# One ring of four PSUM banks, scores through SBUF and grouped exponentials in an attention and two-layer kernel on one Trainium2 core

## The chip, the core and the metric

The kernel runs on one core of a Trainium2 chip. A core has five engines that run side by side, each with its own queue of instructions in a fixed order: PE (matrix products, into PSUM), ACT (activation functions), DVE (elementwise and reductions), POOL (elementwise, SBUF only) and SP, which here only issues DMAs. PSUM has eight banks of 128 x 512 floats. The metric is the device time of one execution in microseconds, the median of the runs shown; less is better.

## What is computed

Landmark attention for 4 batches of 8 heads (576 tokens, head size 64, 32 landmarks), then two dense layers on its 2304 x 512 output:

```python
A  = softmax(q @ k_lm^T / 8)      # 576 x 32 for each head
Bm = softmax(q_lm @ k_lm^T / 8)   # 32 x 32
C  = softmax(q_lm @ k^T / 8)      # 32 x 576
Z  = Bm^T / (norm1(Bm) * norminf(Bm))
for _ in range(6): Z = 2 * Z - Z @ Bm @ Z
x  = A @ Z @ C @ v                # q_lm, k_lm: means over 18 tokens
h  = x @ w_in;  x = (h * cos(h)) @ w_out             # 512 -> 2048 -> 512
h  = x @ w_in2; out = (max(h, 0) + alpha * min(h, 0)) @ w_out2
```

## The kernel before, in words

**A planner sets the order.** Every step is entered with `op(...)`: the engines that may do it, its buffers, an optional due time. `Plan.go` then places all steps by its own table of durations; where a step may go to two engines (a copy to ACT or DVE, a subtraction to POOL or DVE) it chooses. A step whose function table on ACT (`aset`: "exp" or "sin") is not the loaded one costs it 1.28 more and a later due time. The result is a fixed order on each engine. Buffers of one tag form a ring: a new one waits until the one that many places ahead in the ring is done with.

**Attention.** A batch is two units of four heads (`unit`, names `u0`, `u1` for batch 0, `U2` to `U7` after it). For each unit: k, q and v are loaded (batches 1 to 3 into `raw`, a ring of three that the loads of the layers' weights share); k and q are transposed on PE (L594); landmark sums go on POOL (L646) and are written into `kq`. The scores of C (L670 into two banks, 320 and 256 columns) are reduced to a maximum on DVE (L685, L687), and ACT takes their exponential straight from PSUM in two instructions (L692). C is transposed (L700, L704), copied to SBUF (L318 on ACT or L320 on DVE) and multiplied with v (L715). The scores of A (L670 too) are transposed by DVE (L742), reduced (L747), subtracted, sent through the exponential (L749), normalised and split into a hi and a lo part (L455, L323). `z_path` does Bm, its exponential (L800), and five Newton steps (L851 on PE, L853 on DVE) for the whole batch; its result `wt`, times `w_in`, gives V' (L909, hi part L911, lo part L912).

**First layer, a tick at a time.** Batch, half (288 tokens) and a slice of 128 of the 2048 columns make one of 128 ticks. A tick is six h1 products (L949) into one bank of tag `h`; ACT rounds (L954), DVE takes the rest (L956), ACT takes Sin (L958) and Square (L959), DVE multiplies by h (L960), which frees the bank; then a hi and a lo part (L963, L323) and twelve y1 products (L976) in four groups of three, into `acc`. The hi and lo parts have four buffers, so that h1 is at most some four ticks, 16 groups, ahead of y1. Ticks 0 to 15 belong to batch 0, 16 to 31 to batch 1, 32 to 63 to both again, 64 to 95 to batch 2, 96 to 127 to batch 3. The attention of batches 0 and 1 runs in the prologue, that of batch 2 is entered at tick 36 and that of batch 3 at tick 66. Beside all that DVE converts the weights from 64-bit to 32-bit floats (L471, L473, L475).

**Second layer.** Products by a Strassen scheme (L1235), for the last 256 tokens plain (L1280), and a second product (L1316).

**PSUM.** Tag `h` has two banks (h1, and half of the attention of batch 0), `x` two (the rest of the attention, V'), `acc` four. Sin and the exponential belong to different tables on ACT; each change is an ACT_TABLE_LOAD.

## Time and profile before

| | us |
|---|---|
| median of 3 runs | 882.39 (881.43 to 885.32) |
| the profiled execution | 881.18 |
| its span, first to last instruction | 879.4 |
| busy: PE, DVE, ACT, POOL | 825.8, 646.4, 483.9, 198.2 |

Busy times of an engine are counted per stretch of the span; a stretch in which PE is busy all the time can still hold products that take longer than in another. The rows on which the prediction rests stand in a section of their own below.

### The profile page before, as it was taken

The numbers are of one execution on the slowest core, as the hardware profiler recorded it, in microseconds if no ns is written. First come the engines' busy times: TensorE is split into PE (matmuls) and PEld (weight loads), VectorE is DVE, ScalarE is ACT, GpSimd is POOL, SyncE is SP. The second block draws the span as 40 slices with busy tenths as digits, with TensorE's granted clock in tenths as the row PEclk, the third lists the DMA queues.
The fourth block names the chain that finished last, engine by engine and source line by source line (L and its number), as shares of the span: only waits on it lengthen the run. The fifth ranks groups of instructions, "written<-read, shape, count | busy, mean of one in ns | idle before, by whom it ended". The sixth has DMA issues, their size and how long they took to land.

```text
span 879.4 us, 15395 instructions
## 1 busy us (share of the span) xinstructions
PE 825.8 (94%) x5681; PEld 726.3 (83%) x5681; DVE 646.4 (74%) x1279; ACT 483.9 (55%) x1118; POOL 198.2 (23%) x220
## 2 busy tenths in 40 slices
PE   5677899999999998999989999999999999999997
PEld 4436789888798887897889888889999999999996
DVE  4989969987896889768998777775665566555563
ACT  4467757777875687667678534443344334333431
POOL 1224511333321332114432222200120012000110
PEclk8989999999999999999999999999999999999999
DMA  8476506775359846666555111140113011310231
GB/s 233 116 215 143 171 26 189 229 178 136 123 159 268 230 119 196 186 182 218 182 185 181 51 48 48 61 132 25 37 61 85 25 37 60 85 37 25 66 115 24
DMA packets 89051, 107.44 MB, mean 122 GB/s; under 512 B 35984, under 2 KB 63120, under 8 KB 88976
## 3 DMA queue, kind: packets, MB, share of 16 engines
q1 hardware_dynamic: 88976, 106.46, 41.2%
q8 instruction: 44, 0.72, 0.3%
q14 instruction: 31, 0.25, 0.1%
HBM read 82.06 MB, written 24.38 MB: 121 GB/s over the span
## 4 chain that ended last, share of the span: by engine, by line
PE 61%; DVE 19%; DMA 10%; issue 3%; ACT 3%; SPq 1%; POOL 1%; DVEq 0%; POOLq 0%; ACTq 0%
PE acc L1316 21%; PE acc L976 10%; PE h L1235 9%; PE x L1235 7%; PE h L949 5%; DMA m<-in_moe_w_in_dram 4%; DMA m<-in_moe_w_out_dram 3%; DVE m L323 3%; DVE m L475 3%; DVE m L473 3%; PE x L909 2%; DMA m<-wi2d 2%; DVE m L471 2%; DVE m L960 2%; DVE m L956 2%
## 5 line engine op out<-in xcount | busy, mean ns | idle before, releaser
L976 PE MATMUL acc<-m,m 128*128 128x288 f32 x1536 | 238.0, 301 | 7.0 <-DVE m L323 3.4
L323 POOL TENSOR_TENSOR m<-m,m 128x288 fp32r<-128x288 f32 (+3 forms) x129 | 126.0, 984 | 459.7 <-ACT m L963 233.5
L976 PEld LDWEIGHTS acc<-m,m 128*128 128x128 f32 x1536 | 213.7, 190 | 18.4 <-issue 7.7
L1316 PE MATMUL acc<-m,m 128*128 128x512 f32 x864 | 207.5, 392 | 0.7 <-DVE m L323 0.4
L323 DVE TENSOR_TENSOR m<-m,m 128x512 fp32r<-128x512 f32 (+4 forms) x271 | 170.3, 651 | 34.9 <-ACT m L1184 9.3
L1316 PEld LDWEIGHTS acc<-m,m 128*128 128x128 f32 x864 | 158.9, 189 | 31.9 <-DVE m L323 0.9
L949 PE MATMUL h<-m,m 128*128 128x288 f32 x768 | 131.8, 307 | 14.9 <-DVE m L960 12.8
L949 PEld LDWEIGHTS h<-m,m 128*128 128x128 f32 x768 | 109.6, 191 | 34.9 <-DVE m L960 19.9
L1304 ACT ACTIVATE m<-m 128x512 fp32r<-128x512 f32 (+1 forms) x80 | 46.3, 588 | 111.5 <-DVE m L1302 109.0
L1235 PE MATMUL h<-m,m 128*128 128x256 f32 x768 | 106.9, 282 | 0.7 <-ACT m L318 0.6
L1235 PEld LDWEIGHTS h<-m,m 128*128 128x128 f32 x768 | 99.7, 189 | 3.6 <-ACT m L318 1.3
L1258 DVE TENSOR_TENSOR m<-h,m 128x512 f32<-128x512 f32 x32 | 22.1, 690 | 81.8 <-ACT m L318 78.9
L1235 PE MATMUL x<-m,m 128*128 128x256 f32 x576 | 80.3, 283 | 1.7 <-ACT m L318 1.7
L963 ACT ACTIVATE m<-m 128x288 fp32r<-128x288 f32 x128 | 55.8, 441 | 40.5 <-DVE m L960 35.4
L1235 PEld LDWEIGHTS x<-m,m 128*128 128x128 f32 x576 | 73.1, 188 | 3.4 <-ACT m L318 1.9
L318 ACT ACTIVATE m<-h 128x256 f32<-128x256 f32 (+2 forms) x93 | 36.8, 396 | 67.2 <-PE h L1235 58.9
L958 ACT ACTIVATE m<-m 128x288 f32<-128x288 f32 x128 | 55.6, 440 | 26.4 <-DVE m L956 26.0
L960 DVE SCALAR_TENSOR_TENSOR m<-m,h 128x288 f32<-128x288 f32 x128 | 56.5, 446 | 15.1 <-ACT m L959 14.8
L1095 ACT ACTIVATE m<-m 128x512 fp32r<-128x512 f32 x68 | 41.4, 628 | 45.0 <-PE h L1235 19.4
L954 ACT ACTIVATE m<-h 128x288 int32<-128x288 f32 x128 | 51.4, 404 | 22.8 <-PE h L949 22.0
L956 DVE SCALAR_TENSOR_TENSOR m<-h,m 128x288 f32<-128x288 f32 x128 | 57.0, 448 | 3.4 <-ACT m L954 3.2
L959 ACT ACTIVATE m<-m 128x288 f32<-128x288 f32 x128 | 55.2, 439 | 2.4
(150 smaller groups left out, 897.5 us busy)
## 6 DMA issues: line engine op xcount, KB each, us to landing
m<-in_moe_w_in_dram SPq DMA_DIRECT2D x32, 512.0 KB, 5.4
m<-in_moe_w_out_dram SPq DMA_DIRECT2D x32, 512.0 KB, 4.4
m<-wi2d SPq DMA_DIRECT2D x56, 256.0 KB, 3.5
...
```

What stands on the lines that cost most here:

```text
L323: ENG[e].tensor_tensor(o, a, b, op=ALU.subtract)
L949: nc.tensor.matmul(out=hp.t[:, 0:CW], lhsT=w_[:, js], rhs=x[:, cs], start=(i == 0), stop=(i == 5))
L954: op(act(CW, True), lambda e: nc.scalar.activation(k_.t, hp.t[:, 0:CW], AF.Copy, scale=INV2PI), r=[hp], w=[k_], target=T + 0.8)
L956: op(dve(CW), lambda e: nc.vector.scalar_tensor_tensor(u.t, hp.t[:, 0:CW], INV2PI, k_.t, op0=ALU.mult, op1=ALU.subtract), r=[hp, k_], w=[u])
L958: op(act(CW), lambda e: nc.scalar.activation(u.t, u.t, AF.Sin, scale=math.pi), rw=[u], aset="sin")
L959: op(act(CW), lambda e: nc.scalar.activation(u.t, u.t, AF.Square, scale=math.sqrt(2.0)), rw=[u])
L960: op(dve(CW), lambda e: nc.vector.scalar_tensor_tensor(hc.t, u.t, 1.0, hp.t[:, 0:CW], op0=ALU.subtract, op1=ALU.mult, reverse0=True), r=[h ...
L963: op(act(CW), lambda e: nc.scalar.activation(gh.t, hc.t, AF.Copy), r=[hc], w=[gh, gl])
L976: nc.tensor.matmul(out=yg[o].t[:, 0:CW], lhsT=w_.t[:, sl], rhs=x.t, start=(j == ja and i == 0), stop=(j == jb and i == 2),)
L1235: nc.tensor.matmul(out=rv(k), lhsT=a_.t[:, p, c2, js], rhs=b_.t[:, q_, c2, 0:hw], start=(first and c2 == 0 and i == 0), stop=(c2 == 1 and ...
L1304: op(act(w), lambda e, m_=m_, gh=gh: nc.scalar.activation(gh.t[:, 0:w], m_.t[:, 0:w], AF.Copy), r=[m_], w=[gh, gl])
L1316: nc.tensor.matmul(out=ya[n][t].t, lhsT=gv(x_), rhs=r_.t, start=(st and k == 0), stop=(en and k == 2))
```

## The change

Four things are edited.

1. **PSUM.** Tags `h` and `x` become one tag `h` with four banks. The C scores and A scores of batch 0 stay in `acc`.
2. **C scores of batches 1 to 3.** Each of the two score banks is copied to SBUF (ACT or DVE) into `ce`; one reduction on DVE then takes the negated maximum of all 576 columns (L703 in the new file) and one ACT instruction the exponential in place (L705). `ce` of these batches has two buffers in place of one; for that `wt` has two in place of four.
3. **Two groups of exponentials.** For each batch from 1 on, the exponential of C of the first unit waits for the maximum of the second and for the subtraction in `z_path`; that of C of the second waits for the first; that of A of the first waits for A's subtraction in the second. v of the first unit is loaded after k and q of both.
4. **The planner.** A step that needs the other table and is not overdue gets 1.0 added to the key by which it is chosen (`SP`).

```diff
 KN = dict(..., AG=8, SP=1.0, KA=0.004, KC=25, DRY=0)
...
                     key = s + KA * min(dl - s, KC)
+                    if o.aset and o.aset != cur and o.dl > s:
+                        key += KN["SP"]
...
-    at = at_raw = lay(0, at, ("wt", 4, 1024))
+    at = at_raw = lay(0, at, ("wt", 2, 1024), ("cex", 1, CE))
...
-    for tag, n in (("h", 2), ("x", 2), ("acc", 4)):
+    place["1ce"] = (1, CE, place["1ce"][2] + place.pop("cex")[2])
+    for tag, n in (("h", 4), ("acc", 4)):
...
-        bank = (lambda i: psb("hx"[i & 1])) if m == 0 else (lambda i: psb("x"))
-        pair = (lambda: (psb("acc"), psb("acc"))) if m == 0 else (lambda: (psb("x"), psb("x")))
+        bank = (lambda i: psb("h")) if m == 0 else (lambda i: psb("h"))
+        pair = (lambda: (psb("acc"), psb("acc"))) if m == 0 else (lambda: (psb("h"), psb("h")))
...
-        loads(4, ldv, 1.64, w=[vn], after=aft)
+        marks["vl", b, c] = loads(4, ldv, 1.64, w=[vn], after=aft)
...
+            if m:
+                ce = ce or atb(m, "ce", [P, R0, 2, 64])
+                op(pe(n, 4), cs, r=[kt, kqb[p][1]], w=[sc[ch]])
+                op([act(n, True), dve(n)], lambda e, ch=ch, n=n: copy(
+                    e, ce.t[:, 0:n // 64, ch, :], sc[ch].t[:, 0:n].rearrange("p (r s) -> p r s", s=64)),
+                   r=[sc[ch]], w=[ce])
+                continue
...
+            marks["cn", b, c] = op(dve(S), lambda e: nc.vector.tensor_reduce(
+                nm_.t, ces(), axis=AX.X, op=ALU.max, negate=True), r=[ce], w=[nm_])
+            marks["ce", b, c] = op(("ACT", S / 1200.0 + 0.18), lambda e: nc.scalar.activation(
+                ces(), ces(), AF.Exp, bias=nm_.t, accum_out=sm.t[:, 0:1]), r=[nm_], rw=[ce], w=[sm], aset="exp")
...
-        pv = psb("x")
+        pv = psb("h")
...
         z_path(b, tick_time(s + KN["UZ"]))
+        marks["vl", b, 0].after += gates["ld"]
+        marks["ce", b, 0].after += [marks["cn", b, 1], marks["zs", b]]
+        marks["ce", b, 1].after += [marks["ce", b, 0]]
+        marks["et", b, 1].after += [marks["et", b, 0]]
+        marks["vl", b, 1].after += [marks["vl", b, 0]]
+        marks["ae", b, 0].after += [marks["as", b, 1]]
         gates["v"] = [g.ops[-1]]
...
-        X, Y = psb("h"), psb("x")
+        X, Y = psb("h"), psb("h")
```

What the planner makes of it is shown at three places. In the rows L numbers are lines of each file's own; in the new file L705 and L774 are the exponentials of C and A, L825 that of z, L979, L983, L984 and L988 rounding, Sin, Square and hi part of a tick, L936 the hi part of V', L320 copies, L974 and L1001 h1 and y1.

ACT, before, near tick 50, from the second unit's C (L692) to z's exponential (L800) and on to A's (L749):

```order
L692 ACT_TABLE_LOAD
L692 ACTIVATE m_175,m_69<-x,m_69 128x5x64
L692 ACTIVATE m_175,m_69<-x,m_69 128x4x64
L954 ACTIVATE m_479<-h 128x288
L958 ACT_TABLE_LOAD
L958 ACTIVATE m_479<-m_479 128x288 x2
L959 ACTIVATE m_479<-m_479 128x288 x2
L318 ACTIVATE m_157<-x 64x128
L800 ACT_TABLE_LOAD
L800 ACTIVATE m_69<-m_69 128x64
L911 ACTIVATE m_1253<-x 128x512
```

The first unit's exponentials stood some six ticks ahead of these, between loads of their own. ACT, after, in the same place:

```order
L705 ACT_TABLE_LOAD
L705 ACTIVATE m_170,m_69<-m_170,m_69 128x576
L774 ACTIVATE m_69<-m_69 128x576
L705 ACTIVATE m_434,m_69<-m_434,m_69 128x576
L825 ACTIVATE m_69<-m_69 128x64
L774 ACTIVATE m_69<-m_69 128x576
L936 ACTIVATE m_1269<-h 128x512 x2
L983 ACT_TABLE_LOAD
L983 ACTIVATE m_483<-m_483 128x288
L459 ACTIVATE m_447<-m_1107 128x576
L984 ACTIVATE m_483<-m_483 128x288
L320 ACTIVATE m_69<-m_69 32x2x32 x4
```

All five exponentials of the batch stand in one piece, and the copies of C's transposes (128x512) stand behind the last row. In the whole order the table loads go from 24 to 12: from 6 to 8 in the prologue, from 10 to 2 near tick 50, from 8 to 2 near tick 80.

PE, before, behind h1 of ticks 79 and 80 (L779 is z's product, L700 and L704 the transposes of C, L670 scores, L715 C times v):

```order
L779 MATMUL x<-m_69 32x32 x8
L976 MATMUL acc<-m_504,m_1795 128x288 x3
L700 MATMUL x<-m_69,m_175 128x128 x4
L976 MATMUL acc<-m_504,m_1795 128x288 x6
L704 MATMUL x<-m_69,m_175 64x128
L976 MATMUL acc<-m_504,m_1795 128x288 x6
L670 MATMUL x<-m_175,m_69 64x320 x2
L670 MATMUL x<-m_175,m_69 64x256 x2
L976 MATMUL acc<-m_504,m_1795 128x288 x6
L715 MATMUL x<-m_157 32x64 x20
```

PE, after, behind h1 of tick 80 (L804 is z's product, L721 and L725 the transposes of C, L674 scores, L736 C times v):

```order
L1001 MATMUL acc<-m_519,m_1830 128x288 x3
L674 MATMUL h<-m_170,m_69 64x320 x2
L674 MATMUL h<-m_170,m_69 64x256 x2
L1001 MATMUL acc<-m_519,m_1830 128x288 x12
L804 MATMUL h<-m_69 32x32 x8
L1001 MATMUL acc<-m_519,m_1830 128x288 x33
L721 MATMUL h<-m_69,m_170 128x128 x4
L725 MATMUL h<-m_69,m_170 64x128
```

The y1 products that stood between the steps of the attention now stand ahead of the transposes; behind these come h1 of tick 81, C times v, h1 of tick 82, and the second unit's transposes.

SP, before, the loads of batch 1 in the prologue (ring `raw`):

```order
L465 DMA m_157<-in_moe_w_out_dram 128x1024
L568 DMA m_157<-in_v_dram 64x2x320
L569 DMA m_157<-in_v_dram 64x2x256
L568 DMA m_157<-in_v_dram 64x2x320
L569 DMA m_157<-in_v_dram 64x2x256
L465 DMA m_157<-in_moe_w_out_dram 128x1024
L552 DMA m_157<-in_k_dram 64x9x64 x4
L465 DMA m_157<-in_moe_w_out_dram 128x1024
L552 DMA m_157<-in_q_dram 64x9x64 x4
```

SP, after:

```order
L469 DMA m_152<-in_moe_w_out_dram 128x1024 x2
L556 DMA m_152<-in_k_dram 64x9x64 x4
L469 DMA m_152<-in_moe_w_out_dram 128x1024
L556 DMA m_152<-in_q_dram 64x9x64 x4
L572 DMA m_152<-in_v_dram 64x2x320
L573 DMA m_152<-in_v_dram 64x2x256
L572 DMA m_152<-in_v_dram 64x2x320
L573 DMA m_152<-in_v_dram 64x2x256
```

The first unit's v has moved behind the second unit's k and q.

## Rows read from the trace of the kernel before

**Rows 1.** The page: its head, and PE's busy time.
```profile
span 879.4 us, 15395 instructions
PE 825.8 (94%) x5681; PEld 726.3 (83%) x5681; DVE 646.4 (74%) x1279; ACT 483.9 (55%) x1118; POOL 198.2 (23%) x220
```
**Rows 2.** Busy times by stage: stretch, length, engines, PE clock, DMA share, GB/s.
```profile
47.00:130.00 83.00, 68.73 (x496) 54.52 (x494) 69.72 (x149) 52.70 (x123) 28.61 (x29) 0.94 0.49 134
130.00:191.90 61.90, 59.84 (x418) 54.00 (x416) 58.66 (x115) 45.80 (x117) 16.72 (x14) 1.00 0.63 190
191.90:228.30 36.40, 35.92 (x294) 31.22 (x294) 25.84 (x60) 28.86 (x67) 16.17 (x23) 1.00 0.57 146
228.30:251.00 22.70, 21.78 (x193) 17.91 (x192) 21.91 (x61) 20.49 (x43) 4.26 (x6) 1.00 0.36 111
251.00:276.30 25.30, 25.13 (x181) 23.36 (x180) 20.68 (x46) 16.17 (x41) 5.74 (x7) 1.00 0.76 237
276.30:336.00 59.70, 57.61 (x431) 48.14 (x430) 47.75 (x98) 41.30 (x96) 18.56 (x26) 1.00 0.73 198
336.00:377.60 41.60, 37.71 (x305) 34.10 (x305) 34.94 (x89) 28.48 (x68) 7.98 (x9) 1.00 0.56 180
377.60:478.90 101.30, 96.05 (x662) 87.54 (x663) 85.41 (x159) 73.63 (x187) 36.92 (x38) 0.98 0.60 194
478.90:879.40 400.50, 392.28 (x2468) 354.78 (x2466) 247.54 (x425) 155.16 (x335) 52.84 (x52) 1.00 0.19 57
```
**Rows 3.** The chain at ticks 118 to 125: start, us, what.
```profile
460.77 1.60 PE acc L976 x12
462.38 0.80 PE h L949 x6
```
**Rows 4.** The same chain, batch 3's attention: dense pieces of PE.
```profile
295.36 0.66 PE x L594 x6
...
300.49 1.87 PE x L909 x8
...
304.55 1.12 PE x L670 x8
...
310.24 0.44 PE x L700 x4
...
313.69 0.88 PE x L715 x40
...
351.96 0.72 PE x L851 x4
```
**Rows 5.** ACT by line, 191.9 to 377.6 us: busy, mean ns, idle before.
```profile
L318 ACT ACTIVATE m<-x 128x384 f32<-128x384 f32 (+3 forms) x26 | 11.6, 471 | 2.9 <-PE x L594 1.2 <-PE x L878 1.1 <-PE x L700 0.5
L958 ACT ACT_TABLE_LOAD x9 | 11.5, 1283 | 0.2
...
L692 ACT ACTIVATE m<-x,m 128x320 f32<-128x320 f32 (+1 forms) x8 | 3.9, 497 | 0.0
...
L318 ACT ACTIVATE m<-m 32x64 f32<-32x64 f32 x11 | 2.8, 254 | 0.5 <-DVE m L825 0.3
L749 ACT ACTIVATE m<-m 128x576 f32<-128x576 f32 x4 | 2.7, 686 | 0.1
L692 ACT ACTIVATION_READ_ACCUMULATOR m<-x,m 128x1 f32 x8 | 1.6, 196 | 0.0
```
**Rows 6.** DVE by line, whole run: the reductions of A and C.
```profile
L747 DVE TENSOR_REDUCE m<-m 128x18 f32<-128x576 f32 x8 | 5.9, 743 | 0.1
...
L685 DVE TENSOR_REDUCE m<-x 128x1 f32<-128x320 f32 (+1 forms) x12 | 5.2, 450 | 0.9 <-PE x L670 0.8
```
**Rows 7.** SP's issues in the prologue, in order of time: start, us, what.
```profile
81.88 0.33 SPq L465 DMA_DIRECT2D m<-in_moe_w_out_dram  x1
82.32 2.98 SPq L552 DMA_DIRECT2D m<-in_q_dram  x4
```
**Rows 8.** Waits of PE, whole run: total us, times, longest.
```profile
PE h L949 <- DVE m L960: 12.8, 18, 3.6
```

More of the change, by code (lines that the diff above doesn't have):

```diff
@@ L674, in scores @@
             )
-        sc = pair()
-        mx, nm_, sm = atb(m, "cmx", [P, 2]), atb(m, "cnm", [P, 1]), atb(m, "csm", [P, 2])
+        sc = pair() if m == 0 else (psb("h"), psb("h"))
+        mx = None if m else atb(m, "cmx", [P, 2])
+        nm_, sm = atb(m, "cnm", [P, 1]), atb(m, "csm", [P, 2])
+        ce = None
         for ch in range(2):
@@ L686, in unit, with ces @@
                r=[sc[ch]], w=[mx])
-        op(dve(2), lambda e: nc.vector.tensor_reduce(nm_.t, mx.t, axis=AX.X, op=ALU.max, negate=True),
-           r=[mx], w=[nm_])
-        ce = atb(m, "ce", [P, R0, 2, 64])
-        for ch in range(2):
-            n = (N0, N1)[ch]
-            op(("ACT", n / 1200.0 + 0.18), lambda e, ch=ch, n=n: nc.scalar.activation(
-                ce.t[:, 0:n // 64, ch, :], sc[ch].t[:, 0:n].rearrange("p (r s) -> p r s", s=64),
-                AF.Exp, bias=nm_.t, accum_out=sm.t[:, ch:ch + 1]), r=[sc[ch], nm_], w=[ce, sm], aset="exp")
+        if m:
+            def ces():
+                return ce.t.rearrange("p r t s -> p (r t s)")[:, 0:S]
+            marks["cn", b, c] = op(dve(S), lambda e: nc.vector.tensor_reduce(
+                nm_.t, ces(), axis=AX.X, op=ALU.max, negate=True), r=[ce], w=[nm_])
+            marks["ce", b, c] = op(("ACT", S / 1200.0 + 0.18), lambda e: nc.scalar.activation(
+                ces(), ces(), AF.Exp, bias=nm_.t, accum_out=sm.t[:, 0:1]), r=[nm_], rw=[ce], w=[sm], aset="exp")
+        else:
+            op(dve(2), lambda e: nc.vector.tensor_reduce(nm_.t, mx.t, axis=AX.X, op=ALU.max, negate=True),
+               r=[mx], w=[nm_])
+            ce = atb(m, "ce", [P, R0, 2, 64])
+            for ch in range(2):
+                n = (N0, N1)[ch]
+                op(("ACT", n / 1200.0 + 0.18), lambda e, ch=ch, n=n: nc.scalar.activation(
+                    ce.t[:, 0:n // 64, ch, :], sc[ch].t[:, 0:n].rearrange("p (r s) -> p r s", s=64),
+                    AF.Exp, bias=nm_.t, accum_out=sm.t[:, ch:ch + 1]), r=[sc[ch], nm_], w=[ce, sm], aset="exp")
         e1, e2 = bank(0), bank(1)
@@ L722, in unit @@
         rs = atb(m, "crs", [P, 2])
-        op(dve(2), lambda e: nc.vector.scalar_tensor_tensor(
-            rs.t[:, 0:1], sm.t[:, 0:1], 1e-9, sm.t[:, 1:2], op0=ALU.add, op1=ALU.add), r=[sm], w=[rs])
+        if m:
+            op(dve(2), lambda e: nc.vector.tensor_scalar_add(rs.t[:, 0:1], sm.t[:, 0:1], 1e-9), r=[sm], w=[rs])
+        else:
+            op(dve(2), lambda e: nc.vector.scalar_tensor_tensor(
+                rs.t[:, 0:1], sm.t[:, 0:1], 1e-9, sm.t[:, 1:2], op0=ALU.add, op1=ALU.add), r=[sm], w=[rs])
         op(dve(2), lambda e: nc.vector.reciprocal(rs.t[:, 1:2], rs.t[:, 0:1]), rw=[rs])
@@ L740, in unit @@
             o1 = op(pe(n, 4), asc, r=[qt, kqb[p][0]],
-               w=[sa[ch]] if ch else [*sa, at], after=[o1] if ch else [])
+               w=[sa[ch]] if ch else [sa[ch], at] if m else [*sa, at], after=[o1] if ch else [])
             op(dve(n), lambda e, ch=ch, n=n, sa=sa, at=at: nc.vector.transpose(
@@ L761, in z_path @@
     def z_path(b, tz):
-        bank = (lambda i: psb("hx"[i & 1])) if b == 0 else (lambda i: psb("x"))
+        bank = (lambda i: psb("h")) if b == 0 else (lambda i: psb("h"))
         cs = [b % 2]
```

20 lines of the change are left out of this document (11 added, 9 removed).

## The prediction

> **What bounds the kernel now.** I read the page first [rows 1]: PE is busy for 825.8 of 879.4 us. Then the busy times by stage [rows 2], cut at the first h1 matmul of a tick. The prologue (0 to 130 us: attention of batches 0 and 1, ticks 0 to 15) has PE at 68.7 of its last 83.0 us; DVE, at 69.7, and the raw ring on SP pace it. From 130 us on PE is the bound almost everywhere. The second layer (478.9 to 879.4) is PE throughout, 392.3 of 400.5 us.
>
> A busy PE hides stretched matmuls, so I price PE's work by dense pieces. In the undisturbed end of the first layer a tick is 0.80 us of h1 and 1.60 us of y1 [rows 3], 2.40 us in all, or 0.40 for each of the four groups of three y1 matmuls. In the attention [rows 4]: one V' half 0.94 (1.87 for two), three transposes 0.33, one pair of score products 1.12, the transposes of C 0.44, C times v 0.88, one Newton step 0.72. A unit is then 1.98 + 2.24 + 0.44 + 0.88 = 5.5, and a batch, with five Newton steps (3.6) and about 1 us of small products, 15.7 us.
>
> Against that, stage by stage:
> - B, ticks 16 to 39: 24 x 2.40 + 5 x 0.94 = 62.3; it took 61.9.
> - C, ticks 40 to 63 (attention of batch 2): 24 x 2.40 + 6 x 0.94 + 15.7 = 78.9; it took 36.4 + 22.7 + 25.3 = 84.4, so 5.5 over.
> - D, ticks 64 to 91 (batch 3): 28 x 2.40 + 6 x 0.94 + 15.7 = 88.5; it took 59.7 + 41.6 = 101.3, so 12.8 over.
> - E, ticks 92 to 126, with no attention at all: 35 x 2.40 + 8 x 0.94 = 91.5; it took 101.3, so 9.8 over.
>
> So C and D together lose 18.3 us, and that is all that a better attention can win there. E loses as much per us without it. The direct wait for a bank (h1 for L960, which frees the h bank) is 12.8 us in the whole run, in 18 waits of 3.6 us at most [rows 8].
>
> **The change, part by part.**
>
> *Table loads.* The order holds 24 before and 12 after: in C 10 become 2, in D 8 become 2, in the prologue 6 become 8. In C and D that is 14 x 1.283 = 18.0 us of ACT's time [rows 5]. ACT is at 28.9 of 36.4 and 41.3 of 59.7 us there [rows 2], below PE, so these are not 18 us of the end: they count only where a tick's Sin waits behind them. The Trainium skill (page "ScalarE: Activation LUTs", section "Table sets: the hidden batching unit") has the rule to do all functions of one set before the next; by that rule alone the change can only gain. It is a rival below.
>
> *Scores through SBUF (batches 1 to 3).* A unit drops two exponentials of 0.497 + 0.196 us for one over 576 columns, taken as A's exponential of that size, 0.686, plus 0.196: 0.5 us less on ACT. It adds two copies out of PSUM; in C and D all eight stand on ACT, at the 0.47 of L318's group about 0.9 us a unit [rows 5]. DVE drops two maxima of 0.45 for one over SBUF of the size of L747's, 0.743 [rows 6]: 0.2 less. These sums cancel to within 1 us a batch, beside work of PE. What changes is when banks come free: the score banks after a copy rather than after the exponential.
>
> *Until the grouped exponentials.* No table load lies in ticks 40 to 49 or 64 to 79 any more, and h1 has four banks. PE's row there in the new order: ticks 40 to 49 hold 10 x 0.80 + 40 x 0.40 + 2 V' + 36 transposes + four score pairs = 8.0 + 16.0 + 1.9 + 4.0 + 4.5 = 34.4; with 1 us of loss 35.4 against 36.4: 1 gained. Ticks 64 to 79 hold 12.8 + 64 x 0.40 + 6 V' + 36 transposes + three score pairs = 12.8 + 25.6 + 5.6 + 4.0 + 3.4 = 51.4; with 2 us of loss 53.4 against 59.7: 6.3 gained, of which about 3 is PE work that now comes later.
>
> *At the grouped exponentials.* Here the gain is paid for. At tick 80 the new ACT order has, in a row: load, C, A, C, the small one of z, A, load, then Sin of tick 80. That is 1.28 + 0.88 + 0.69 + 0.88 + about 0.25 + 0.69 + 1.28 = 6.0 us in which no tick moves. Behind the Sin stand, before the copy that C's transposes wait for, a hi half, Square, four copies of y1 and four small ones: with the copy eight at about 0.47 and four at 0.254, 4.8 us. So C times v on PE comes about 0.69 + 0.88 + 0.25 + 0.69 + 1.28 + 4.8 = 8.6 us after the first C exponential, where PE has one h1 (0.80) left to do before it: a stall near 7 us. In the order of before that copy stands two or three instructions behind its exponential. Queued behind the waiting product on PE are h1 of ticks 82 and 83, the second unit's transposes and z; behind ACT's copies, Sin of tick 81. The transposes' two banks and those of h1 80 and 81 fill the ring, so h1 82 can't start earlier. Cover for the stall is the y1 backlog, at most 16 groups, 6.4 us, and the order spends all of them ahead of the transposes. DVE has the softmax of two units and z in one piece there too, and the hc of tick 80 stands behind them. I put ticks 80 to 91 at 47.5 us against 41.6 (PE's own pieces 9.6 + 48 x 0.40 + about 9 = 38, plus 7 of stall, plus 2.5 of Newton steps waiting for DVE): 6 lost. Bounds: 2, if copies and Sin come as early as their inputs allow, and 8. In C at tick 50 the block is longer by two V' copies, but PE has two V' halves and the second y1 part for it: ticks 50 to 54 lose 2 (bounds 0 and 4), and ticks 55 to 63, which inherit 4 groups and two Newton steps (3.0 us) and lose less themselves, another 1.
>
> D: -6.3 + 6 = -0.3, C: -1 + 2 + 1 = +2. I lower both by 1 us for the four banks, since a Sin that is late no longer holds the next but one h1: D -1.5, C +1.
>
> *The prologue.* SP's order moves unit 3's q load ahead of unit 2's v load. Before, a weight load waited for v's buffer until 81.88 us and q, queued behind it, was issued at 82.32 [rows 7]. In the new order q waits for a weight conversion instead; I put it 5 us earlier (bounds 0 and 7). Against that the exponentials of batch 1 now wait for both units and for z, two more loads (2.6 us) lie on that chain, and C times v of unit 3 comes before the Newton steps, with both units' softmax on DVE ahead of them: 2 to 8 us later from the product of z on. PE holds more y1 in that wait (64 groups done at tick 16, 57 before; 7 x 0.40 = 2.8). Together 5 + 2.8 - 5 = about 2.5 gained, bounds 6 gained and 4 lost; ticks 16 to 39 then refill an empty backlog, 1 to 2 us, which I count within these bounds.
>
> *E and F.* From tick 92 on both orders are nearly the same, row for row from the second layer on. Nothing there.
>
> Sum: C +1, D -1.5, prologue -2, in all -2.5 on 881.2, the profiled execution's own time (span 879.4 and 1.8 around it): 878.7. The median of the runs stands 1.2 higher: 879.9. I forecast **880**, no difference that can be told (about 0.5%, 4.4 us).
>
> **The rivals.**
> 1. *The group is hidden* (faster). ACT loses 16 us of work in C and D and the four banks let h1 run ahead, so PE's stall at ticks 50 and 80 shrinks to the lower bounds: at tick 80 2 lost instead of 6, C 1 gained, the prologue 5 gained. -6.3 + 2 - 1 - 5 = -10.3: 872. For it: over C and D DVE is busy 151.1 and ACT 135.3 of 185.7 us, so both have room [rows 2]. Against it: the static order puts the copies behind the Sin whatever the load.
> 2. *Every load removed counts* (faster). If each removed load ended a wait of PE, 12 x 1.283 = 15.4 us: 867. This is what the Trainium skill's rule on batching by table set would make of it. PE loses only 5.5 us in C, where eight loads go, which speaks against it.
> 3. *The ring fills* (slower). Scores, V', transposes, z and h1 share four banks; a bank held behind the grouped exponentials stops h1 altogether. Place: ticks 50 and 80, and C times v of unit 3 in the prologue. It decides once the time in which no tick moves (6.0 plus the copies, 10.8) exceeds the 6.4 us of y1 left at the group's start. Price: 8 in ticks 80 to 91, 6 in ticks 50 to 63, 2 in the prologue, against 7.3 gained in ticks 40 to 49 and 64 to 79: +8.7, 891.
> 4. *The moved q load gains nothing* because DVE's conversions pace it anyway: the forecast loses 2.5: 882.5, still no difference.
>
> **How the numbers follow.** Forecast, with 4 in it, 0.41; rival 1 0.28; rival 2 0.05; rival 3 0.26. Faster by over 0.5% (below 878): 0.28 + 0.05 + 0.03 of the forecast's lower end, 0.36. Slower (above 886.8): 0.26. The rest, 0.38, is within. The range reaches from rival 1 with its bounds to rival 3: 870 to 891; the forecast's own is 876 to 886.
>
> **What would show it.** 12 table loads; ticks 64 to 79 near 53 us; ticks 80 to 91 near 47 with an idle PE of several us before L736 (C times v), released by ACT's copy; h1 waiting little for L985. q of unit 3 issued near 77 us, and tick 16 starting at 128 to 132. Wrong if PE shows no stall at tick 80 (rival 1), or if ticks 40 to 63 take over 88 us (rival 3).

## The result: 1.5% slower, and the prologue is where

The changed kernel took 895.55 us (median; 894.61 to 896.61) against 881.91 us of the kernel before, run on the same chip: a ratio of 1.0148, 95% interval 1.0119 to 1.0177. The forecast was 880 us, no difference, in a range of 870 to 891. The prediction was wrong.

The page of the changed kernel, its head and the busy times of the engines (for before see [rows 1]):

```profile
span 894.8 us, 15351 instructions
...
PE 831.3 (93%) x5681; PEld 732.4 (82%) x5681; DVE 640.7 (72%) x1256; ACT 472.5 (53%) x1112; POOL 201.4 (23%) x225
```

The busy sums say little: ACT has 11.4 us less work, as the change meant, and PE is busy 5.5 us longer with the same 5681 matmuls. The stages say more. Columns as in [rows 2], each stretch cut at the first h1 matmul of ticks 0, 16, 40, 50, 55, 64, 80, 92 and 127:

```profile
47.60:145.50 97.90, 76.83 (x508) 59.61 (x506) 71.04 (x152) 55.78 (x121) 30.07 (x31) 0.87 0.40 115
145.50:203.50 58.00, 57.44 (x406) 52.74 (x405) 54.09 (x110) 43.30 (x112) 14.29 (x14) 1.00 0.62 189
203.50:240.70 37.20, 35.31 (x259) 30.38 (x257) 27.00 (x52) 26.15 (x68) 16.51 (x24) 1.00 0.61 145
240.70:262.30 21.60, 19.57 (x215) 16.35 (x213) 20.93 (x61) 16.31 (x38) 5.88 (x6) 1.00 0.29 92
262.30:290.70 28.40, 28.38 (x196) 25.90 (x195) 22.07 (x48) 16.15 (x42) 6.15 (x7) 1.00 0.73 229
290.70:344.60 53.90, 52.99 (x374) 45.26 (x373) 40.26 (x76) 35.49 (x91) 18.66 (x27) 1.00 0.73 193
344.60:391.30 46.70, 41.37 (x365) 38.98 (x364) 40.00 (x101) 30.54 (x76) 10.08 (x11) 0.93 0.49 163
391.30:494.40 103.10, 95.17 (x664) 87.33 (x663) 84.28 (x157) 73.26 (x187) 37.61 (x38) 0.98 0.64 207
494.40:894.80 400.40, 391.84 (x2468) 354.69 (x2466) 247.30 (x424) 154.78 (x334) 52.52 (x52) 0.99 0.19 58
```

Against [rows 2]: tick 40 starts at 203.5 in place of 191.9, so **11.6 of the 15.4 us are lost before it**. Ticks 40 to 63 take 87.2 (84.4 before, +2.8), ticks 64 to 91 100.6 (101.3, -0.7), ticks 92 to 126 103.1 (101.3, +1.8), the rest 400.4 (400.5).

By tick 40 both kernels have done the same work, 914 matmuls from tick 0 on. PE's idle time there is (97.9 - 76.8) + (58.0 - 57.4) = 21.7 us against 14.3 + 2.1 = 16.4, so 5.3 more; its busy time is 134.3 against 128.6, so 5.7 more for the same instructions, at a mean granted clock of 0.87 against 0.94 up to tick 16. Of the 11.0 us more from tick 0 to tick 40, idle time and longer busy time are each half.

**What stands in the way there.** The chain of waits of the changed kernel, 90 to 145 us (start, us, what):

```profile
103.43 1.28 ACT L983
104.73 0.44 ACT m L983
105.19 1.28 ACT L705
106.48 1.63 ACT m L705 x4
...
109.79 1.62 PE h L736 x39
111.41 0.30 SPq L469
...
112.46 3.75 DMA m<-in_v_dram
116.24 0.96 DVE m L475
...
119.88 1.34 DVE m L325
121.26 7.86 PE acc L1001 x37
129.12 0.65 PE h L876 x4
```

Read downward: a Sin between two table loads (L983), then the grouped exponentials of C (L705); only then C times v of unit 2 (L736), which is the last reader of that unit's v. v stands in one of three raw buffers, and with its end SP issues the weight load L469 at 111.4. SP's own row shows that this load had stood in its queue for 21 us (the x2 are the seventh w_out slice, issued at 90.0, and the eighth):

```profile
90.01 21.70 SPq L469 DMA_DIRECT2D m<-in_moe_w_out_dram  x2
```

The eighth slice is what y1 of tick 7 needs, and all y1 behind it; it is converted from 116.2 (L475) and split at 119.9 (L325), and 37 y1 matmuls follow from 121.3. In the kernel before, the eighth slice, also the last w_out load ahead of unit 3's v, was issued at 94.2:

```profile
94.21 0.33 SPq L465 DMA_DIRECT2D m<-in_moe_w_out_dram  x1
```

PE's rows, 107 to 131 us (start, us, what, in brackets the idle time before and who ended it), and DVE's:

```profile
107.40 1.12 PE L721 MATMUL h<-m,m 128*128 128x128 f32 x4 [3.88 <-ACT m L705]
...
114.32 2.66 PE L974 MATMUL h<-m,m 128*128 128x288 f32 x18
116.91 0.31 PE L736 MATMUL h<-m 128*32 128x64 f32 x4
...
119.90 0.53 PE L1001 MATMUL acc<-m,m 128*128 128x288 f32 x2 [1.36 <-ACT m L459]
121.26 7.86 PE L1001 MATMUL acc<-m,m 128*128 128x288 f32 x37 [0.84 <-DVE m L325]
128.96 0.81 PE L876 MATMUL h<-m 128*128 128x192 f32 x4
```
```profile
109.63 0.42 DVE L864 TENSOR_TENSOR m<-h,m 128x256 f32<-128x256 f32 x1 [0.38 <-PE h L862]
...
127.80 0.81 DVE L985 SCALAR_TENSOR_TENSOR m<-m,h 128x288 f32<-128x288 f32 x2
```

The operand of the first Newton step is there at 110.05 (L864), yet the step (L876) runs at 128.96, 19 us later. In the kernel before, the operand (L839 there) was there at 113.44 and the step (L851) ran at 113.58:

```profile
113.02 0.42 DVE L839 TENSOR_TENSOR m<-x,m 128x256 f32<-128x256 f32 x1
```
```profile
113.58 0.89 PE L851 MATMUL x<-m 128*128 128x192 f32 x4
```

In the changed kernel no row shows the step itself waiting: the fixed order of PE has it behind the 37 y1 products. By the order of the ring the planner could not put it earlier. After h1 of ticks 13 to 15 (the 18 matmuls at 114.3) and C times v, the step is the fifth in a ring of four and takes the bank of tick 13. That is read last by L985, at 127.80, whose outputs wait for y1 to free their buffers, and y1 waits for the slice. So the one ring ties the attention of batch 1 to h1, h1 to y1, y1 to a weight load, and the load to the attention. This is read off the rows; whether it is the cause, the runs had to say.

**At tick 80** the foreseen stall is there, in PE's rows and in its waits (whole run: total, times, longest):

```profile
350.61 4.65 PE L1001 MATMUL acc<-m,m 128*128 128x288 f32 x33
...
360.44 1.55 PE L736 MATMUL h<-m 128*32 128x64 f32 x40 [3.84 <-ACT m L320]
```
```profile
PE h L736 <- ACT m L320: 4.0, 2, 3.8
...
PE h L974 <- DVE m L985: 1.8, 4, 0.8
```

### The profile page after: what moved, and what is told of

The parts are those of the page before. It is cut to its first block, busy times and chain, and to the rows that moved or that the text cites. A ratio compares the mean times of both kernels' runs of the same rounds, so it can differ in the third digit from the quotient of the medians.

```text
span 894.8 us, 15351 instructions
## 1 busy us (share of the span) xinstructions
PE 831.3 (93%) x5681; PEld 732.4 (82%) x5681; DVE 640.7 (72%) x1256; ACT 472.5 (53%) x1112; POOL 201.4 (23%) x225
## 4 chain that ended last, share of the span: by engine, by line
PE 67%; DVE 13%; DMA 9%; ACT 5%; issue 2%; SPq 2%; POOL 1%; DVEq 0%; ACTq 0%; POOLq 0%
PE acc L1347 20%; PE h L1266 16%; PE acc L1001 15%; PE h L974 6%; DMA m<-in_moe_w_out_dram 3%; DVE m L325 3%; DMA m<-in_moe_w_in_dram 3%; PE h L1311 3%; PE h L934 2%; DVE m L477 2%; DVE m L479 2%; DMA m<-wi2d 2%; DVE m L475 1%; PE h L876 1%; ACT m L320 1%
## 5 line engine op out<-in xcount | busy, mean ns | idle before, releaser
L1001 PE MATMUL acc<-m,m 128*128 128x288 f32 x1536 | 237.6, 302 | 17.2 <-DVE m L325 6.1
L1001 PEld LDWEIGHTS acc<-m,m 128*128 128x128 f32 x1536 | 216.5, 192 | 24.0 <-DVE m L325 7.2
L325 POOL TENSOR_TENSOR m<-m,m 128x288 fp32r<-128x288 f32 (+4 forms) x129 | 124.1, 969 | 467.1 <-ACT m L988 206.5
L325 DVE TENSOR_TENSOR m<-m,m 128x512 fp32r<-128x512 f32 (+4 forms) x271 | 171.5, 655 | 40.7 <-ACT m L988 11.0
L1266 PEld LDWEIGHTS h<-m,m 128*128 128x128 f32 x1344 | 166.1, 189 | 6.9 <-ACT m L320 3.1
L1266 PE MATMUL h<-m,m 128*128 128x256 f32 x1344 | 168.5, 283 | 2.5 <-ACT m L320 2.5
L974 PE MATMUL h<-m,m 128*128 128x288 f32 x768 | 130.8, 306 | 6.9 <-DVE m L937 3.5
L974 PEld LDWEIGHTS h<-m,m 128*128 128x128 f32 x768 | 110.5, 191 | 25.8 <-DVE m L937 7.3
L320 ACT ACTIVATE m<-h 128x256 f32<-128x256 f32 (+3 forms) x180 | 71.7, 415 | 93.0 <-PE h L1266 73.7
L1289 DVE TENSOR_TENSOR m<-h,m 128x512 f32<-128x512 f32 x64 | 41.7, 685 | 82.2 <-ACT m L320 79.3
L988 ACT ACTIVATE m<-m 128x288 fp32r<-128x288 f32 x128 | 56.4, 442 | 52.5 <-DVE m L985 46.9
L983 ACT ACTIVATE m<-m 128x288 f32<-128x288 f32 x128 | 56.2, 441 | 33.2 <-DVE m L981 32.6
L985 DVE SCALAR_TENSOR_TENSOR m<-m,h 128x288 f32<-128x288 f32 x128 | 57.0, 447 | 15.9 <-ACT m L984 15.5
L979 ACT ACTIVATE m<-h 128x288 int32<-128x288 f32 x128 | 51.6, 403 | 29.9 <-PE h L974 28.0
L984 ACT ACTIVATE m<-m 128x288 f32<-128x288 f32 x128 | 56.1, 440 | 2.4
L479 DVE SCALAR_TENSOR_TENSOR m<-m,m 128x512 int32<-128x512 int32 x64 | 52.3, 823 | 0.3
L475 DVE TENSOR_SCALAR m<-m 128x512 int32<-128x512 int32 x64 | 34.3, 538 | 22.4 <-DMA m<-in_moe_w_in_dram 12.0
```

Of the source, the lines that this page charges most:

```text
L320: nc.scalar.activation(o, i, AF.Copy)
L325: ENG[e].tensor_tensor(o, a, b, op=ALU.subtract)
L479: op(dve(512), lambda e: nc.vector.scalar_tensor_tensor(cf.t, rv(0), 29, cf.t, op0=ALU.logical_shift_right, op1=ALU.bitwise_or), r=[raw], ...
L974: nc.tensor.matmul(out=hp.t[:, 0:CW], lhsT=w_[:, js], rhs=x[:, cs], start=(i == 0), stop=(i == 5))
L983: op(act(CW), lambda e: nc.scalar.activation(u.t, u.t, AF.Sin, scale=math.pi), rw=[u], aset="sin")
L984: op(act(CW), lambda e: nc.scalar.activation(u.t, u.t, AF.Square, scale=math.sqrt(2.0)), rw=[u])
```

## The experiments

Eighteen kernels. Each was timed beside the kernel before on the same chip; "ratio" is against that. "tick 16" and "tick 40" are the times at which these ticks start, read from PE's h1 rows, the next three columns the lengths of the stretches in us, "loads" the table loads. Tick 0 starts between 46.8 and 49.0 us, but at 50.6 in e12 and at 53.3 in e14.

Ticks and stretches come from one profiled execution of each kernel, the ratio from 4 to 10 executions. The executions of the kernel before that were timed here lie between 879.3 and 888.8 us, so a difference of a few us in one stretch can be the execution's and not the kernel's.

| kernel | tick 16 | tick 40 | 40-63 | 64-91 | 92-126 | loads | ratio (95%) |
|---|---|---|---|---|---|---|---|
| before | 130.0 | 191.9 | 84.4 | 101.4 | 101.3 | 24 | 1 |
| changed | 145.5 | 203.5 | 87.2 | 100.6 | 103.1 | 12 | 1.0148 (1.0119-1.0177) |
| e1 | 145.3 | 206.2 | 86.2 | 100.4 | 102.9 | 10 | 1.0181 (1.0143-1.0218) |
| e2 | 144.9 | 203.6 | 91.2 | 101.4 | 104.6 | 24 | 1.0222 (1.0189-1.0255) |
| e3 | 130.7 | 196.1 | 87.0 | 104.4 | 102.4 | 8 | 1.0128 (1.0092-1.0163) |
| e4 | 156.9 | 217.3 | 86.5 | 100.1 | 102.3 | 10 | 1.0300 (1.0260-1.0340) |
| e5 | 146.6 | 207.4 | 94.0 | 101.3 | 106.2 | 22 | 1.0324 (1.0281-1.0366) |
| e6 | 139.0 | 202.6 | 89.5 | 98.8 | 104.2 | 8 | 1.0135 (1.0093-1.0176) |
| e7 | 134.4 | 200.8 | 85.8 | 97.7 | 102.6 | 16 | 1.0063 (1.0042-1.0085) |
| e8 | 139.5 | 205.1 | 87.2 | 101.8 | 103.0 | 8 | 1.0177 (1.0109-1.0245) |
| e9 | 133.4 | 199.1 | 88.3 | 99.2 | 101.5 | 24 | 1.0047 (1.0023-1.0071) |
| e10 | 134.4 | 198.9 | 86.1 | 101.9 | 104.8 | 20 | 1.0146 (1.0117-1.0175) |
| e11 | 144.6 | 209.7 | 85.7 | 100.2 | 104.5 | 10 | 1.0177 (1.0140-1.0214) |
| e12 | 141.5 | 200.0 | 92.3 | 103.6 | 104.6 | 8 | 1.0188 (1.0141-1.0235) |
| e13 | 135.7 | 196.9 | 84.5 | 101.7 | 102.4 | 26 | 1.0038 (1.0018-1.0059) |
| e14 | 132.1 | 197.0 | 82.7 | 98.2 | 102.9 | 8 | 1.0020 (1.0000-1.0041) |
| e15 | 127.4 | 192.0 | 83.6 | 100.6 | 102.5 | 22 | 0.9952 (0.9927-0.9978) |
| e16 | 126.1 | 193.4 | 85.1 | 98.7 | 102.0 | 12 | 0.9992 (0.9969-1.0015) |
| e17 | 136.2 | 202.2 | 82.9 | 103.2 | 102.7 | 24 | 1.0062 (1.0045-1.0079) |
| e18 | 135.6 | 195.9 | 89.2 | 104.4 | 102.3 | 8 | 1.0109 (1.0091-1.0126) |

### Is it the grouping? (e1, e2)

e1 leaves the marks of batch 1 away, e2 all of them:

```diff
+        if b > 1:                    # e1; e2 drops the lines
             marks["ce", b, 0].after += [marks["cn", b, 1], marks["zs", b]]
             ...
```

> The changed kernel without the waits that group the exponentials (and v loads and transposes) of batch 1; batches 2 and 3 stay grouped. Theory T (the 11.5 us that the changed kernel has lost by tick 40 come from the grouping of batch 1, which lets C times v of unit 2, and so the buffer of its v, and so the w_out loads behind it, wait): unit 2's C times v is done before 100, no gap of 21 us between weight loads on SP's queue between 90 and 111, tick 16 starts at 128 to 135 (145.5 in the changed kernel, 130.0 before), and the whole takes 880 to 889 us, with 18 to 20 table loads. Rival R1 (the one ring of four banks holds PE): tick 16 stays at 141 to 147, whole 892 to 897. Rival R2 (the groups at ticks 50 and 80 cost the time): whole 893 to 897.

> The changed kernel without any of the waits that group (batches 1, 2 and 3); the ring of four and the scores through SBUF stay. Theory T: tick 16 at 128 to 135; beyond that ticks 80 to 91 lose the stall before C times v and come back from 46.7 to 41 to 43 us while ticks 64 to 79 stay near 54 if their gain is the ring's, or go back to 58 to 60 if it is the grouping's; whole 878 to 887. Rival R1 (ring): tick 16 at 141 to 147, whole 890 to 897. Rival R2 (the groups of batches 2 and 3 cost it): whole at least 5 us under the run that ungroups batch 1 alone.

Measured: 898.56 and 901.70 us, and tick 16 at 145.3 and 144.9. Theory T falls: the prologue loses the same without the groups. R1, the ring, has tick 16 right in both, though the whole came out above its range. The eighth w_out slice is late in both all the same (issued at 105.0 and 104.8), held by other tenants of the raw buffers. With one ring the groups even help: without them ticks 40 to 63 take 91.2 us. R2 falls with T.

### Is it the ring? (e3, e5, e7)

e3 gives the changed kernel its two rings back; e5 puts one ring into the kernel before; e7 is e3 without the groups.

```diff
-    for tag, n in (("h", 4), ("acc", 4)):
+    for tag, n in (("h", 2), ("x", 2), ("acc", 4)):      # e3, e7; e5 the other way
```

> The changed kernel with the two rings of two banks of before (h apart from attention and V'), grouping and scores through SBUF kept. Theory T: the prologue's loss stays, tick 16 at 141 to 148, and ticks 64 to 79 lose part of their gain (55 to 60 us against 53.9): whole 893 to 903. Rival R1 (the shared ring lets h1 and attention stand in each other's way): tick 16 back at 128 to 135 and the whole at 880 to 887.

> The kernel before with nothing changed but its two rings of two banks, made one ring of four for h, attention and V'. Theory T3 (in the prologue the h1 of up to four ticks, which need batch 0 alone, sit in all four banks until their squares are multiplied, and that waits for y1 and its weights; transposes, scores and the Newton steps of batch 1 wait for a bank meanwhile): the first Newton step comes at 122 or later (113.6 before), tick 16 at 140 to 147 (130.0 before), tick 40 at 198 to 205 (191.9), and the whole at 886 to 897. Rival R5 (the ring costs only together with the grouping or the scores through SBUF): tick 16 at 128 to 134, whole 878 to 885.

> The changed kernel with two rings of two banks and without the waits that group: what is left of the change is the scores through SBUF. T3: tick 16 at 128 to 134. With the two rings and the groups tick 40 stood at 196.1, 4.1 us behind the kernel before: if the groups of batch 1 cost that, tick 40 is at 190 to 194 here; if the scores through SBUF do, it stays at 195 to 198. Ticks 80 to 91 at 41 to 44 without the group's stall (48.9 with two rings and groups). Whole 882 to 888 in the first case, 887 to 893 in the second.

Measured: 892.87, 911.29 and 888.23 us. The ring alone makes the kernel before 3.2% slower, far over what T3 had said, and it loses in every stage of the first layer but ticks 64 to 91. Its prologue is like that of the changed kernel: SP's row shows the eighth slice late again (106.9), and PE's row y1 waiting for it, here for 6.65 us in one piece. The first Newton step comes at 132.5.

```profile
113.63 5.71 PE L976 MATMUL acc<-m,m 128*128 128x288 f32 x27 [6.65 <-ACT m L455]
```
```profile
106.91 0.34 SPq L465 DMA_DIRECT2D m<-in_moe_w_out_dram  x1
```

With two rings in the changed kernel (e3) tick 16 stands at 130.7 again, and the first Newton step at 113.99 although the eighth slice is late there too (104.7).

```profile
113.99 0.81 PE L876 MATMUL x<-m 128*128 128x192 f32 x4
```

So the ring is what couples the Newton steps to y1. But the whole hardly moves (1.0128 against 1.0148): tick 40 comes 7.4 us earlier and ticks 64 to 91 take 3.8 longer. The parts do not add up: with the groups the time is 0.65% longer with two rings (e3 against e7) and 0.74% shorter with one (changed against e2). The section "Each small part alone, and no part at all" shows that differences of this size also come from a new order alone, so neither is shown to be a cost or a gain of the groups. And e7, which has neither ring nor groups, has tick 40 at 200.8, later than e3 with its groups and in neither of its cases. Beside the scores it still holds the planner's price for a table change, which e9 takes out.

### Can one link of the loop be cut? (e4, e6, e8, e11, e12)

e4 loads v of unit 2 behind the sixth w_out slice; e6 holds h1 to two banks in ticks 2 to 15 (e8 in all ticks); e11 loads q of unit 3 behind the eight slices, in the order of their use; e12 is e6 and e11.

```diff
+            marks["vl", b, 0].after.append(cvops[13])                       # e4, b == 1
-                     after=[h1op[s - 1]] if s else [])
+                     after=... + ([free_[s - 2]] if 2 <= s < 16 else []))   # e6; free_[s] is L985 of tick s
+                if u == 3 and nm == "qn":
+                    aft = aft + cvops[12:16]                               # e11
```

> The changed kernel with every group kept, and one more wait: v of unit 2 is loaded after the sixth w_out slice, so that it takes the raw buffer of no w_out slice of the first eight. Theory T by the buffer: the eighth w_out slice is issued before 100 (111.4 in the changed kernel), y1 from tick 7 on doesn't stop for it, tick 16 at 128 to 136, whole 880 to 890. Rival T2 (it is not the buffer: the grouped exponentials hold the z chain and C themselves, and V' waits for those): the eighth slice early but tick 16 still at 140 to 147, whole 890 to 897.

> The changed kernel with one rule more for the order: in ticks 2 to 15, h1 of a tick is put after the product (1 - u) h of the tick two before it, so that h1 holds at most two banks of the one ring in the prologue. Theory T3: the first Newton step by 118 (129.0 in the changed kernel), tick 16 at 128 to 136, tick 40 at 194 to 199 (203.5), everything behind as in the changed kernel, whole 885 to 891. Rival R6 (the late eighth w_out slice alone sets it, whatever the banks): tick 16 stays at 140 to 147, whole 892 to 897.

> As the run that holds h1 to two banks in ticks 2 to 15, but in every tick from 2 on. It tells what the one ring gives from tick 64 on: ticks 64 to 79 take 57 to 60 us if their gain (59.7 before, 53.9 in the changed kernel) comes from h1 running ahead into free banks, and 53 to 56 if it comes from more banks for attention and V'. Tick 16 at 128 to 136 by T3, 140 to 147 by R6. Whole 885 to 897.

> The changed kernel with one load order more: q of unit 3 is loaded after the eight w_out slices of the first ticks, and these in the order in which y1 needs them. Ring and groups stay. Theory T4 (the loss by tick 40 is PE without y1's weights, 21.6 us of idle time between tick 0 and tick 40 against 16.3 before, and the lower clock that follows): y1 waits for no w_out slice after 85, idle PE between tick 0 and tick 40 at 14 to 18, tick 40 at 193 to 199 (203.5), whole 885 to 891. Rival (q of unit 3 later makes the z product, the Newton steps and V' of batch 1 later by as much): tick 16 at 146 to 152, tick 40 at 202 to 208, whole 893 to 900.

> Both: h1 of ticks 2 to 15 held to two banks, and the eight w_out slices loaded ahead of q of unit 3. If banks and weights are the two causes of the prologue's loss: tick 16 at 128 to 134, tick 40 at 192 to 196, whole 884 to 888. If neither is (the order that the planner finds is worse by itself): tick 40 stays at 200 to 205, whole 892 to 897.

Measured: 908.50, 894.81, 898.33, 900.17 and 901.19 us. e6 shows that the banks held by h1 are a real link: the first Newton step comes 10 us earlier than in the changed kernel, tick 16 6.5 us earlier.

```profile
119.18 1.65 PE L876 MATMUL h<-m 128*128 128x192 f32 x4
```

But tick 40 moves by 0.9 us only. The eighth slice is still issued at 107.7, and PE has 21.9 us idle by tick 40, as in the changed kernel. e11 cuts the other link: the last of the eight slices is issued at 87.8, y1 waits 1.2 us for a weight's hi half and no more between 80 and 145, and tick 40 comes at 209.7, since q of unit 3 is now late (issued at 91.7, 80.5 in the changed kernel) and the Newton steps run at 129.9 to 137.0, PE waiting 0.65 us for four of the five. PE's idle time by tick 40 is 26.7 us there, and not the 14 to 18 of its theory. e4 is worse, and its edit did not do what it was meant to: the eighth slice is issued at 113.4, not before 100, so it doesn't decide between its theories. Three waits of y1 for a weight's hi half take 18.4 us. e12 trades the wait of y1 for one of the transposes (L600 there). The waits of PE in e4 and in e12:

```profile
PE acc L1001 <- ACT m L459: 18.4, 3, 9.3
```
```profile
PE h L600 <- DVE m L325: 8.8, 1, 8.8
```

The absolute times hide what e12 gives: its tick 0 starts 3 us after that of the changed kernel, and from tick 0 to tick 40 it takes 149.4 us, where the changed kernel takes 155.9 and the kernel before 144.9. Its stages 0 to 16 and 16 to 40:

```profile
50.60:141.50 90.90, 72.28 (x512) 57.10 (x510) 67.80 (x144) 53.70 (x128) 27.00 (x29) 0.88 0.50 127
141.50:200.00 58.50, 56.29 (x403) 52.16 (x402) 55.85 (x110) 42.73 (x111) 13.58 (x14) 1.00 0.60 187
```

It loses that again behind tick 40 (ticks 40 to 63 take 92.3 us). e8, with h1 in two banks throughout, was to tell what the ring gives from tick 64 on: its ticks 64 to 79 take 55.1 us, the case in which the gain there is not h1 running ahead into free banks.

So links of the loop can be cut, and each cut opens another wait. None of the five met its theory's case for the prologue and the whole; e11 and e12 came nearer to their rivals'. What these runs share with the changed kernel is that the planner laid the whole order anew with numbers (TA, VE, AB and the rest) that were those of the kernel before.

### Each small part alone, and no part at all (e9, e10, e13, e17)

e9 has only the scores through SBUF (two rings, no groups, planner's price at 0); e10 is the kernel before with only the planner's price for a table change; e13 and e17 are the kernel before with no part of the change and one planner number moved by 5 and by 10%.

```diff
-KN = dict(... AB=0.2, ... KA=0.004, ...)
+KN = dict(... AB=0.19, ... KA=0.004, ...)     # e13
+KN = dict(... AB=0.2, ... KA=0.0044, ...)     # e17
```

> Two rings of two banks, no waits that group, and the planner's price for a table change (SP) at 0: of the change only the scores through SBUF are left. The run with the price at 1 had tick 40 at 200.8 (191.9 before) and ticks 64 to 91 in 97.7 us (101.4 before). If the price costs the 8.9 us by tick 40: tick 40 at 190 to 195, whole 877 to 883. If the scores through SBUF cost them: tick 40 at 198 to 203, whole 886 to 891. Ticks 64 to 91 at 96 to 100 in both, if that gain is the scores'.

> The kernel before with the planner's price for a table change (SP = 1) and nothing else of the change. If the price costs the time by tick 40: tick 40 at 197 to 203, whole 886 to 892. If the scores through SBUF do: tick 40 at 190 to 194, whole 879 to 885. Table loads 14 to 20 (24 before).

> The kernel before with one of the planner's numbers moved: AB, by which ScalarE is favoured for an operation that may go on two engines, 0.19 in place of 0.20. No part of the change is in it, and the work is the same but for which engine makes some copies. Theory N (the order of before is a find of the planner's numbers for that program; any alteration loses it): tick 16 at 133 to 140, tick 40 at 196 to 202 (191.9 before), whole 886 to 893. If the parts of the change themselves cost the prologue: tick 40 at 190 to 194, whole 879 to 885.

> The kernel before with another of the planner's numbers moved: KA, the weight of an operation's due time, 0.0044 in place of 0.0040. No part of the change is in it. If the order of before is a find that any alteration loses: tick 40 at 195 to 202 (191.9 before, 196.9 with AB moved), whole 885 to 893. If the first nudge was an unlucky one: tick 40 at 190 to 194, whole 880 to 885.

Measured: 887.01, 895.19, 887.14 and 890.73 us, and tick 40 at 199.1, 198.9, 196.9 and 202.2. By its cases e9 says that the scores cost the time and e10 that the price does, which were meant to exclude each other: each alone loses 7 us by tick 40. e10 is the most telling of the four: the price changes only what the planner chooses, not the work, and its 1.0146 is as much as the whole change costs and more than its own case said (886 to 892 us). Half of it comes behind tick 40. e13 and e17 say why that need not be a cost of the part: with nothing of the change, 5.0 and 10.3 us are lost at the same place. Stages 0 to 16 and 16 to 40, e13 and e17:

```profile
47.30:135.70 88.40, 72.71 (x508) 56.71 (x506) 72.04 (x160) 53.69 (x120) 23.36 (x25) 0.92 0.51 131
135.70:196.90 61.20, 58.45 (x407) 52.51 (x406) 58.89 (x115) 46.07 (x116) 18.74 (x16) 1.00 0.63 186
```
```profile
47.70:136.20 88.50, 73.65 (x508) 57.68 (x506) 71.51 (x161) 53.96 (x120) 23.05 (x25) 0.90 0.51 132
136.20:202.20 66.00, 60.58 (x409) 54.47 (x408) 59.91 (x114) 45.91 (x113) 18.42 (x17) 0.97 0.59 175
```

Here too it is idle time and clock together, 18.4 and 20.3 us of idle PE against 16.4, at 0.92 and 0.90 against 0.94 up to tick 16, without the long stall: the last slice ahead of unit 3's v is issued at 94.8 and 95.5. The prologue of the kernel before is a good find of its numbers, and two of two nudges lose it. (e17's profiled execution, 891.87 us, was the slowest of its four, so its 10.3 us may be on the high side; its ratio is 1.0062.)

### New numbers for each kernel (e14, e15, e16, e18)

e14 is the changed kernel whole, e15 the kernel before, e16 two rings with groups in batch 2 alone, each with planner numbers searched anew (changed at random, kept when the planner's plan grew shorter; no time of a plan is used here). e18 is the changed kernel with one number moved.

```diff
-KN = dict(T0=46, TA=3.4, TBT=3.05, VE=4.0, ... SP=1.0, ...)
+KN = dict(T0=41.0541, TA=3.7632, TBT=2.8949, VE=3.6427, ... SP=0.4538, ...)   # e14
+KN = dict(T0=46, TA=3.74, TBT=3.05, VE=4.0, ... SP=1.0, ...)                  # e18
```

> The changed kernel whole (one ring, scores through SBUF, groups in every batch), with the planner's numbers searched anew for it. Theory N: the prologue's loss goes, tick 16 at 130 to 137, tick 40 at 188 to 196, ticks 40 to 91 as in the changed kernel (188) or a few us under, whole 872 to 884. If the ring has a price of its own in the prologue whatever the order (h1 and the attention of batch 1 in the same four banks): tick 40 at 197 to 204, whole 886 to 896.

> The kernel before with its planner's numbers searched in the same way. It tells what the search is worth by itself, so that the changed kernel with new numbers is compared with its like. If the old numbers are near the best for before: whole 876 to 885, tick 40 at 188 to 193. If the search gives as much as it gives the changed kernel: 866 to 875.

> Two rings of two banks, scores through SBUF, groups for batch 2 alone, with the planner's numbers searched for it. If scores through SBUF are the part that pays (ticks 64 to 91 were 97.7 us with two rings and no groups, 101.4 before): tick 40 at 187 to 193, ticks 64 to 91 at 96 to 100, whole 869 to 880, faster than both kernels. If each part has its own cost in the prologue: tick 40 at 196 to 202, whole 882 to 890.

> The changed kernel with one of the planner's numbers moved: TA, the time that it plans for a tick of the first sixteen, 3.74 in place of 3.4. Ring, groups and scores through SBUF stay whole. If the order that the old numbers give in the prologue is the loss: tick 16 at 134 to 141 (145.5), tick 40 at 195 to 200 (203.5), whole 886 to 892 (895.5). If the ring or the groups hold the prologue whatever the order: tick 16 at 143 to 148, tick 40 at 202 to 206, whole 893 to 898.

Measured: 886.15, 880.17, 882.23 and 894.53 us. e18 gives 7.5 of the 11.6 us by tick 40 back, with ring, groups and scores as they are. Its order puts the last w_out loads ahead of the loads that wait (SP), and the first Newton step at 121.23:

```profile
89.78 3.21 SPq L469 DMA_DIRECT2D m<-in_moe_w_out_dram  x2
```
```profile
121.23 0.81 PE L876 MATMUL h<-m 128*128 128x192 f32 x4
```

It gives most of that back later (ticks 64 to 91 take 104.4 us), and the whole comes to 1.0109 in place of 1.0148; the two intervals overlap. So its prologue met the case of the order, its whole that of the rival. e14, with all numbers new, is level with the kernel before: 1.0020 (1.0000 to 1.0041). Its stages 0 to 16 and 16 to 40:

```profile
53.30:132.10 78.80, 64.81 (x498) 52.87 (x497) 63.47 (x132) 49.45 (x119) 36.83 (x37) 0.94 0.49 142
132.10:197.00 64.90, 60.03 (x420) 55.62 (x419) 59.80 (x106) 46.49 (x120) 29.61 (x27) 0.97 0.65 194
```

From tick 0 to tick 40 it takes 143.7 us, where the kernel before takes 144.9 and the changed one 155.9: the loss there is gone, though tick 0 itself now starts at 53.3 in place of 47.0. By the letter of its cases that put e14 with the rival (tick 40 at 197.0, whole 886.15), by a hair: what is late is tick 0, and from there to tick 40 nothing is left of the loss. Ticks 40 to 91 take 180.9 against 185.8. But the kernel before gains from new numbers too (e15, 0.9952; 143.7 us from tick 0 to tick 40 as well), so with each at the best that was found, the change is still about 0.7% behind (886.15 against 880.17 on the same chip, 10 runs each). The profiled executions of the two, 883.00 and 881.48 us, lie nearer together than that, so the stages don't show where the 0.7% is. e15 is the fastest of all; e16 is level with before, at 882.23 us outside the 869 to 880 that it was to have if the scores pay. No version with a part of the change was shown faster than the kernel before.

## Why the prediction was wrong, point by point

- **The prologue, the step that failed.** The sum had it at -2 (bounds 6 gained, 4 lost); it measured +11.6 by tick 40. q of unit 3 did move, to 80.5 from 82.3 [rows 7], not 5 us but 1.8. The z chain's "2 to 8 us later" was too small for the Newton steps, 129.0 against 113.6, 15 us. And "more y1 in that wait", booked as 2.8 gained, was no cover: the y1 that PE had in its order there had no weights until 119.9. (By the traces 60 groups of y1, not 57, are started before tick 16 in the kernel before and 63 in the changed one: 1.2 us of work, not 2.8.) I priced the two moved instructions and did not follow who holds the raw buffer that the next weight load needs, nor which bank the Newton step takes. Both stood in the order on SP and PE.
- **Whose fault that is.** Not the groups (e1, e2). The ring makes the coupling (e3, e5, e6). But the order decides whether the coupling bites: with the change whole, one number (e18) takes most of the loss away and all of them (e14) what lies between tick 0 and tick 40, and the kernel before loses 5 to 10 us there with no change at all (e13, e17) and 7 with the planner's price alone (e10). The prediction took the order of before as the level from which a change is added and subtracted; it was a favourable one, and a change that makes the planner lay the order anew had some of that to lose. No term stood for it. How the 11.6 us divide between ring and order is not settled: e18 leaves 4.0 of them and e14 5.1, these all ahead of tick 0, and one ring in the kernel before was not tried with numbers of its own.
- **Table loads:** 12, as said. ACT's time fell, and no gain is seen to follow from it: e9 and e2 have 24 loads, e3 has 8, and the times do not rank by them. Rival 2 is out, and the Trainium skill's rule to batch by table set (page "ScalarE: Activation LUTs", section "Table sets: the hidden batching unit") is not seen to gain anything in these runs; ACT is busy for 55% of the span before the change and 53% after it.
- **Ticks 40 to 63:** -1, +2 and +1 before a discount of 1, in sum +1; measured +0.8, -1.1 and +3.1, +2.8. The size of the sum is near, its places are not.
- **Ticks 64 to 79:** 53.4 foreseen, 53.9 measured. Right in size. Four banks for h1, named in the prediction, are not what gives most of it: e3 has 55.5 with two rings and e8 55.1 with h1 in two banks, while e2 has 56.8 without the groups and e5 58.4 with the ring alone. And 4.6 of the 5.8 us gained are busy time of PE, with 57 matmuls fewer in the stretch, where the prediction took about 3 as work that comes later.
- **Ticks 80 to 91:** 47.5 foreseen, 46.7 measured, with the named stall: PE idle before L736 until ACT's copy L320. C times v comes 7.6 us after the end of the first C exponential (at 352.86), where 8.6 was foreseen. But PE then still had y1 until 355.3, and not one h1 alone, so the stall was 3.8 us and not 7. That the sum came near is in part luck: PE is idle for only 1.4 us more than before in the stretch and busy for 3.7 us more, with 60 matmuls more, and the granted clock is 0.93 (1.00 in [rows 2]). Without groups the stretch takes 44.6 (e2).
- **h1 waiting for its bank:** 12.8 us in 18 waits [rows 8] became 1.8 in 4 (L974 for L985). As said, and worth little, since other waits took their place.
- **Ticks 92 to 126:** 0 foreseen, +1.8. Almost the same order there, but not the same time.
- **The rivals.** Rival 3 (the ring fills, slower, 891, chance 0.26) had the sign and one of the places, but put 2 of its 8.7 us into the prologue. Rival 4 was near on the q load (1.8 us earlier) and missed what mattered.
- **Sums.** Three were loose, none by over 1 us: 5 + 2.8 - 5 for the prologue is 2.8, was called 2.5 and entered as 2; D, -0.3 with 1 off, entered as -1.5; and the instructions at 0.47 us from the hi half to the copy are seven, eight only with the Sin itself.
